# Squared norms of keys and queries: the factor goes into the square, and every square is made on ScalarE

## The chip, the cores and the metric

The kernel runs on one core of a Trainium2 chip. The metric is device time in microseconds (us). Three runs of the kernel before took 877.32, 878.21 and 878.77 us; their median, 878.21 us, is the time before. The profile comes from one more execution, which took 880.48 us.

## The reference

Three stages follow each other: attention with random features, and two feed-forward layers on its output.

```
scale = 1 / sqrt(sqrt(64))
q_s, k_s = q * scale, k * scale             # (4, 8, 576, 64)
def phi(x):                                 # omega: (128, 64)
    proj = einsum('bhsd,md->bhsm', x, omega)
    sq = sum(x * x, axis=-1) / 2
    h = proj - sq;  h = h - max(h)
    return exp(h) / sqrt(128)
kv, z = phi(k_s)^T v, sum_s phi(k_s)
x = (phi(q_s) kv) / (phi(q_s) . z + 1e-6)   # to (2304, 512)
h = x w1_in;  g = max(0.01 h, h);  x = g w1_out
h = x w2_in;  g = h * clip(h + 3, 0, 6) / 6;  out = g w2_out
```

What is changed here is `sq`: half of the squared norm of the scaled row, one number per token and head.

## The kernel before, in words

The 2304 tokens are cut into five groups of 512, 256, 512, 512 and 512. Three kinds of work share the engines. Attention comes in units: a key unit or a query unit of one head pair (or of several, for short pieces). The first feed-forward layer (moe1) runs group by group, while the attention of the next group is made beside it. The second layer (moe2) runs at the end; its weights are unpacked and converted earlier, beside the rest. A product of the feed-forward layers is three matmuls, L496, L497 and L498 (high times high, low times high, high times low), since each operand is kept as a high and a low part.

A unit of attention goes like this. DMAs bring the rows twice, transposed (`xT`) and by token (`xn`). TensorE makes the scores from `xT` (L739, L760). `squares` makes the squared norms from `xn`: a square in place (L674 on GpSimd or L675 on ScalarE), a sum over 64 columns on VectorE (L677), and a multiplication by half of scale squared, `halve` (L681, on VectorE or GpSimd). `features` takes the minimum of the scores on VectorE (L704), adds the norm on VectorE (L707), takes it away on VectorE or GpSimd (L710), and ScalarE makes the exponentials with the result as bias (L715). TensorE then makes keys times values (L786 in the first two batches) or transposes and multiplies with the result. The queries of the first group follow `Q_first`: transposes (L853), numerators (L862), a division on VectorE (L867 to L871), a transpose back (L880), and a split into high and low (L883 on ScalarE, L884 on VectorE), which gives the first operand `x` of moe1. Until those four `x` are there, moe1 can't begin. This first stretch, to about 47 us, is called the head below.

The weights come as 64-bit numbers and are turned into 32-bit ones by four steps (L519 or L521, L523, L526, L529), three of them on VectorE, and then split into high and low (L476 or L477, L480 or L481).

No order is written out by hand. `Graph.op` records each operation with a due time, its tiles, and one or more ways to do it: an engine, a cost in nanoseconds and the code. `Graph.run` then plans: at each step it takes the operation that can start first by its own clock of each engine (ties within 60 ns go to the earlier due time), picks for it the way that ends first, and emits it. The engines run what they are given in that order. The costs are those of `c_dve`, `c_act` and `c_pool`; `halve` stands in the table with 71 ns on VectorE and 200 ns on GpSimd. A way that is marked with `True`, or that runs on GpSimd, also holds the planner's clock `port`, one for both engines; `halve` on VectorE is not marked. Where the planner sees TensorE idle in the head for over 0.4 us, it fills half of the gap with matmuls on zeros (L1359, `keep_warm`).

Of the kernel before, what the change touches and what calls it, by code (L numbers as in the profile page):

```python
# [12 lines left out]
AF = mybir.ActivationFunctionType  # L13
ALU = mybir.AluOpType
# [311 lines left out]
def c_dve(n):  # L326
    return n / 0.96 + 69.0
# [6 lines left out]
def c_act(n, psum=False, ap=False):  # L334
    return n / 1.2 + (51.0 if psum else 93.0) + (93.0 if ap else 0.0)


def c_pool(n):
    return n * 2.1 + 147.0
# [11 lines left out]
def attn_moe_kernel(ctx: ExitStack, tc: tile.TileContext, qT, kT, qn, kn, v1, om2, w1i, w1o, w2i, w2o, out):  # L351
# [4 lines left out]
    nc = tc.nc  # L356
    scale = float(D) ** -0.25
    g = Graph()
# [141 lines left out]
    def dma(dst, src, nbytes):  # L500
        return [("sp", c_dma(nbytes), lambda: nc.sync.dma_start(dst(), src))]
# [166 lines left out]
    def squares(ncol, nsrc, due, nh=1):  # L668
        nat, sq = Buf("xn"), Buf("sq")
        N = lambda: nat.tiles[0][:, 0:ncol]  # L670
        to = (lambda: N().rearrange("p (h c) d -> p h c d", h=nh)) if nh > 1 else N
        g.op(dma(to, nsrc, 128 * ncol * 256), wr=[nat], due=due - O2)
        w = ncol * 64
        g.op([("pool", c_pool(w), lambda: nc.gpsimd.tensor_tensor(out=N(), in0=N(), in1=N(), op=ALU.mult)),  # L674
              ("act", c_act(w), lambda: nc.scalar.activation(N(), N(), AF.Square))], wr=[nat], due=due - 3e3)  # L675
        sqc = lambda: sq.tiles[0][:, 0:ncol]
        g.op([("dve", c_dve(w), lambda: nc.vector.tensor_reduce(out=sqc()[:, :, 0], in_=N(), axis=AX.X, op=ALU.add))],  # L677
             rd=[nat], wr=[sq], due=due - 2e3)

        def halve(eng):  # L680
            eng.tensor_scalar(out=sqc(), in0=sqc(), scalar1=0.5 * scale * scale, scalar2=None, op0=ALU.mult)  # L681

        g.op([("dve", 71, lambda: halve(nc.vector)), ("pool", 200, lambda: halve(nc.gpsimd))], wr=[sq], due=due - 2e3)
        return sq

    def exps(raw, h, nm, c, p, due):
# [61 lines left out]
    def K_tail(b, due):  # L748

        sq = squares(HP, kn[b, :, :, 8].rearrange("h p d -> p h d"), due)  # L750
        src, p, h = Buf("xT"), Ps(g.use), Buf("ht")
        last64[b] = h
        g.op(dma(lambda: src.tiles[0][:, 0:HP * 64].rearrange("p (h t) -> p h t", h=HP), kT[b, :, :, 512:576].rearrange(
            "h p t -> p h t"), 128 * HP * 256), wr=[src], due=due - O2)

        def mm():
            for hp in range(HP):
                for e in range(2):
                    r = slice(64 * e, 64 * e + 64)
                    nc.tensor.matmul(p.tiles[0][r, hp * 128:hp * 128 + 128], lhsT=src.tiles[0][r, hp * 64:hp * 64 + 64], rhs=wn[r],  # L760
                                     start=True, stop=True)

        g.op([("pe", HP * 224.0, mm)], rd=[src], wr=[p], also=[h], due=due, mode="S")
        features([p], [h], [HP], [0], sq, due)
# [669 lines left out]
```

## Time and profile before

| what | value |
|---|---|
| median of three runs | 878.21 us |
| the profiled execution | 880.48 us |
| its span, first to last instruction | 878.5 us |
| TensorE matmul busy | 858.8 us (98%) |
| VectorE busy | 688.0 us (78%) |
| ScalarE busy | 486.6 us (55%) |
| GpSimd busy | 195.7 us (22%) |
| mean granted TensorE clock | 0.998 |

The profiled execution took 2.0 us more than its span, which is what lies ahead of the first and behind the last instruction, and 2.27 us more than the median. A busy share says little here by itself: TensorE's matmuls overlap, so that a busy TensorE need not be at its full pace, and the other engines are far busier in the first 350 us, where all of attention lies, than behind it.

### The profile page before, as it was taken

The page shows a single profiled execution, that of the slowest core. Times are in us where ns is not written, and L with a number is a line of the kernel's source. Part 1 is how long each engine was busy: PE and PEld are TensorE (multiplying, and loading weights), DVE is VectorE, ACT ScalarE, POOL GpSimd, SP SyncE. Part 2 cuts the span into 40 slices and gives each one's busy share as a digit, 9 for nine tenths or more (in the row PEclk, how much of TensorE's full clock was granted, in tenths as well). Part 3 has the DMA queues.
Part 4 walks back from the last instruction along what each step waited for, and adds up shares of the span by engine and source line. Part 5 has one row for each costly group of instructions (what it writes and reads, how often), then busy time and mean ns, then how long its engine had stood idle before and what let it go on. Part 6 is the DMA issues. An engine that isn't in the chain of part 4 may idle for free.

```text
span 878.5 us, 17799 instructions
## 1 busy us (share of the span) xinstructions
PE 858.8 (98%) x6339; PEld 781.6 (89%) x6339; DVE 688.0 (78%) x1712; ACT 486.6 (55%) x1132; POOL 195.7 (22%) x334
## 2 busy tenths in 40 slices
PE   8999899999999999999999999999999999999998
PEld 8978787889878878888888888999999999999998
DVE  6999999898998877666688445788678779878865
ACT  7867566676767556554555345544453355445442
POOL 2322222535444412200100001121102303121200
PEclk9999999999999999999999999999999999999999
DMA  9556564668468564799898448884887675677352
GB/s 330 170 174 196 164 209 136 212 210 253 118 183 266 166 192 156 258 372 340 321 355 337 161 150 265 308 303 164 275 292 255 220 268 165 212 261 260 115 160 64
DMA packets 91496, 198.00 MB, mean 225 GB/s; under 512 B 14736, under 2 KB 40976, under 8 KB 91408
## 3 DMA queue, kind: packets, MB, share of 16 engines
q1 hardware_dynamic: 91408, 196.87, 66.6%
q8 instruction: 50, 0.82, 0.4%
q14 instruction: 38, 0.31, 0.1%
HBM read 150.18 MB, written 46.66 MB: 224 GB/s over the span
## 4 chain that ended last, share of the span: by engine, by line
PE 68%; DVE 16%; DMA 7%; ACT 4%; issue 3%; POOL 1%; SPq 1%; DVEq 0%; ACTq 0%; POOLq 0%
PE bank L1062 18%; PE bank L1162 16%; PE bank L496 9%; PE bank L497 9%; PE bank L498 9%; DVE wst L526 2%; DVE nm L704 2%; PE bank L739 2%; DVE junk L910 2%; ACT h L715 2%; DMA late_w<-in 1%; DVE g L1004 1%; DMA third_w<-in 1%; DMA out_raw<-wt 1%; DVE wst L523 1%
## 5 line engine op out<-in xcount | busy, mean ns | idle before, releaser
L1062 PE MATMUL bank<-w,g 128*128 128x256 f32 x720 | 95.9, 275 | 0.5 <-ACT bank L1195 0.3
L1062 PEld LDWEIGHTS bank<-w,g 128*128 128x128 f32 x720 | 87.9, 192 | 1.0 <-ACT bank L1195 0.4
L477 ACT COPY late_u<-bank 128x256 f32<-128x256 f32 (+1 forms) x103 | 39.7, 388 | 86.4 <-PE bank L1162 77.4
L1004 DVE TENSOR_TENSOR g<-bank,g 128x512 fp32r<-128x512 f32 (+1 forms) x80 | 50.9, 637 | 34.7 <-ACT g L477 34.2
L1002 ACT ACTIVATE bank<-bank 128x512 f32<-128x512 f32 (+1 forms) x80 | 44.2, 553 | 55.9 <-PE bank L498 55.8
L715 ACT ACTIVATE h<-bank,nm 128x128 f32<-128x128 f32 x228 | 63.7, 385 | 19.0 <-POOL nm L710 18.7
L496 PE MATMUL bank<-x,w 128*128 128x512 f32 (+1 forms) x180 | 67.0, 372 | 0.3 <-ACT h L715 0.3
L1162 PE MATMUL bank<-x,late_w 128*128 128x256 f32 x528 | 66.7, 275 | 0.0
L496 PE MATMUL bank<-g,w 128*128 128x512 f32 (+1 forms) x180 | 66.7, 371 | 0.0
L498 PE MATMUL bank<-g,w 128*128 128x512 f32 (+1 forms) x180 | 64.7, 359 | 2.0 <-DVE g L1004 1.9
L1162 PE MATMUL bank<-second_w,late_w 128*128 128x256 f32 x474 | 64.7, 275 | 0.9 <-ACT late_u L477 0.5
L497 PE MATMUL bank<-x,w 128*128 128x512 f32 (+1 forms) x180 | 64.5, 358 | 0.0
L498 PE MATMUL bank<-x,w 128*128 128x512 f32 (+1 forms) x180 | 64.5, 358 | 0.0
L497 PE MATMUL bank<-g,w 128*128 128x512 f32 (+1 forms) x180 | 64.5, 358 | 0.0
L1162 PEld LDWEIGHTS bank<-x,late_w 128*128 128x128 f32 x528 | 62.8, 192 | 0.2
L1162 PEld LDWEIGHTS bank<-second_w,late_w 128*128 128x128 f32 x474 | 58.9, 192 | 1.5 <-ACT late_u L477 0.7
L704 DVE TENSOR_REDUCE nm<-bank 128x4 f32<-128x512 f32 (+2 forms) x76 | 48.1, 660 | 3.9 <-PE bank L739 2.8
L710 POOL TENSOR_TENSOR nm<-nm,sq 128x4 f32<-128x4 f32 (+2 forms) x76 | 27.2, 368 | 100.1 <-DVE nm L707 98.2
L921 POOL TENSOR_TENSOR h<-h,den 128x512 f32<-128x512 f32 (+2 forms) x32 | 35.8, 1120 | 52.0 <-DVE den L916 29.7
L496 PE MATMUL bank<-x,second_w 128*128 128x512 f32 (+1 forms) x120 | 44.5, 371 | 1.4 <-ACT h L715 1.4
L480 DVE TENSOR_TENSOR g<-xr,g 128x384 fp32r<-128x384 f32 (+1 forms) x53 | 33.7, 636 | 14.3 <-ACT g L477 13.9
L910 DVE CUSTOM_DVE_ANT_0 junk<-h,zr 128x128 bf16<-128x128 f32 (+1 forms) x128 | 42.8, 374 | 1.0 <-ACT h L715 0.3
(373 smaller groups left out, 2393.6 us busy)
## 6 DMA issues: line engine op xcount, KB each, us to landing
late_w<-in SPq DMA_DIRECT2D x85, 512.0 KB, 4.5
in<-late_w SPq DMA_DIRECT2D x32, 512.0 KB, 4.2
late_w<-in SPq DMA_DIRECT2D x39, 256.0 KB, 5.0
third_w<-in SPq DMA_DIRECT2D x19, 512.0 KB, 4.6
wst<-w2i SPq DMA_DIRECT2D x16, 512.0 KB, 4.5
wst<-w2o SPq DMA_DIRECT2D x16, 512.0 KB, 4.2
x_t<-late_w SPq DMA_DIRECT2D x12, 512.0 KB, 5.3
wst<-w1i SPq DMA_DIRECT2D x10, 512.0 KB, 4.6
```

The lines of the kernel that those rows point to most:

```text
L477: return [("act", c_act(n, psum), lambda: nc.scalar.copy(dst(), src())), dve if psum else dve + (True,)]
L496: nc.tensor.matmul(o, lhsT=ah, rhs=bh, start=start, stop=False)
L497: nc.tensor.matmul(o, lhsT=al, rhs=bh, start=False, stop=False)
L498: nc.tensor.matmul(o, lhsT=ah, rhs=bl, start=False, stop=stop)
L704: g.op([("dve", c_dve(c * 128), lambda raw=raw, n_=n_: nc.vector.tensor_reduce(out=n_()[:, :, 0], in_=raw(), axis=AX.X, op=ALU.min))], rd= ...
L715: nc.scalar.activation(h.tiles[0][:, q * 128:q * 128 + 128], raw()[:, q], AF.Exp, bias=nm.tiles[0][:, q], scale=-1.0)
L910: nc.vector.tensor_tensor_reduce(out=jk.tiles[0][r, q % 2], in0=h.tiles[0][r, q * 128:q * 128 + 128], in1=zr[k].tiles[0][r, e], scale=1.0, ...
L921: eng.tensor_tensor(out=x, in0=x, in1=den.tiles[1][:, 0:c].to_broadcast([128, c, 128]), op=ALU.mult)
L1002: g.op([("act", c_act(n, True), lambda: nc.scalar.activation(P(), P(), AF.Prelu, alpha=0.01))], wr=[p], due=d)
L1004: g.op([("dve", c_dve(n), lambda: nc.vector.tensor_tensor(out=G1(), in0=P(), in1=G0().bitcast(F32), op=ALU.subtract))], rd=[p, (gg, 0)], w ...
L1062: nc.tensor.matmul(acc[bank].tiles[0][:, half * 256:half * 256 + 256], lhsT=src.tiles[x][:, q * 128:q * 128 + 128], rhs=woven(w[k].tiles[y ...
L1162: nc.tensor.matmul(R[r](), lhsT=w[x], rhs=m[y], start=start and k == n == 0, stop=k == 1 and n == 2, skip_group_check=True)
```

## The change

`halve` goes. Its factor, half of scale squared, is taken into the square: ScalarE's activation computes the square of its input times a scale, and the scale is now the root of that factor. The way on GpSimd goes too, since a plain product has no place for the factor, so that all squares are made on ScalarE.

```
-        g.op([("pool", c_pool(w), lambda: nc.gpsimd.tensor_tensor(out=N(), in0=N(), in1=N(), op=ALU.mult)),
-              ("act", c_act(w), lambda: nc.scalar.activation(N(), N(), AF.Square))], wr=[nat], due=due - 3e3)
+        g.op([("act", c_act(w), lambda: nc.scalar.activation(N(), N(), AF.Square, scale=scale * 0.5 ** 0.5))], wr=[nat], due=due - 3e3)
         sqc = lambda: sq.tiles[0][:, 0:ncol]
         g.op([("dve", c_dve(w), lambda: nc.vector.tensor_reduce(out=sqc()[:, :, 0], in_=N(), axis=AX.X, op=ALU.add))],
              rd=[nat], wr=[sq], due=due - 2e3)
-
-        def halve(eng):
-            eng.tensor_scalar(out=sqc(), in0=sqc(), scalar1=0.5 * scale * scale, scalar2=None, op0=ALU.mult)
-
-        g.op([("dve", 71, lambda: halve(nc.vector)), ("pool", 200, lambda: halve(nc.gpsimd))], wr=[sq], due=due - 2e3)
         return sq
```

There are 41 squares. Before, 35 were on ScalarE and 6 on GpSimd; of the 41 `halve`, 10 were on VectorE and 31 on GpSimd. Since the planner's clocks run differently without them, everything from the second pair of units on is planned anew: on TensorE the order is the old one for the first 28 rows of 3375, and again for the last 1701. In the changed kernel, lines from 678 on have numbers that are lower by six (L715 is L709, L862 is L856), and the square and the sum are L674 and L676.

The first place is ScalarE at about 16 us, behind the exponentials of the first query unit (`first_h_5`). `first_xn_0` and `first_xn_1` are the rows by token of the second key unit and of its query unit; `h_0_145` and `h_0_146` are the exponentials of that key unit. Before:

```order
L715 ACTIVATE first_h_5_0_163<-bank_182,nm_0_118 128x128 x4
L675 ACTIVATE first_xn_1_0_169<-first_xn_1_0_169 128x512
L477 COPY zr_0_134<-bank_181 128x256
L521 ACTIVATE first_wt_0_0_174<-first_wst_0_0_172 128x512
L715 ACTIVATE h_0_145<-bank_179,nm_0_119 128x128 x4
L715 ACTIVATE h_0_146<-bank_180,nm_0_120 128x128 x4
```

And now:

```order
L709 ACTIVATE first_h_5_0_163<-bank_182,nm_0_118 128x128 x4
L674 ACTIVATE first_xn_0_0_168<-first_xn_0_0_168 128x512
L477 COPY zr_0_134<-bank_181 128x256
L674 ACTIVATE first_xn_1_0_169<-first_xn_1_0_169 128x512
L521 ACTIVATE first_wt_0_0_174<-first_wst_0_0_172 128x512
L521 ACTIVATE first_wt_1_0_175<-first_wst_1_0_173 128x512
L709 ACTIVATE h_0_145<-bank_179,nm_0_119 128x128 x4
L784 COPY kvf_0_129<-bank_178 128x132
L709 ACTIVATE h_0_146<-bank_180,nm_0_120 128x128 x4
```

The square of `first_xn_0`, which GpSimd made before, now stands here, and a second weight conversion (L521) as well.

The second place is VectorE at the same time: the minima and norms of the two units, and the copies of the first unit's transposes (`first_tq`). Before:

```order
L707 TENSOR_TENSOR nm_0_118<-nm_0_118,sq_0_124 128x4
L677 TENSOR_REDUCE sq_0_125<-first_xn_0_0_168 128x8
L476 COPY first_tq_0_0_171<-bank_177 128x512
L476 COPY first_tq_0_0_171<-bank_178 128x512
L704 TENSOR_REDUCE nm_0_119<-bank_179 128x4
L704 TENSOR_REDUCE nm_0_120<-bank_180 128x4
L867 TENSOR_SCALAR den_0_188<-bank_176 128x4
L707 TENSOR_TENSOR nm_0_119<-nm_0_119,sq_0_125 128x4
```

And now:

```order
L701 TENSOR_TENSOR nm_0_118<-nm_0_118,sq_0_124 128x4
L476 COPY first_tq_0_0_171<-bank_177 128x512
L476 COPY first_tq_0_0_171<-bank_178 128x512
L698 TENSOR_REDUCE nm_0_119<-bank_179 128x4
L698 TENSOR_REDUCE nm_0_120<-bank_180 128x4
L861 TENSOR_SCALAR den_0_188<-bank_176 128x4
L676 TENSOR_REDUCE sq_0_125<-first_xn_0_0_168 128x8
L863 RECIPROCAL den_1_189<-den_0_188 128x4
L676 TENSOR_REDUCE sq_0_126<-first_xn_1_0_169 128x8
L865 TENSOR_TENSOR u_0_116<-bank_176,den_1_189 128x4x64
L861 TENSOR_SCALAR den_0_190<-bank_177 128x4
L701 TENSOR_TENSOR nm_0_119<-nm_0_119,sq_0_125 128x4
```

The sum over `first_xn_0` has moved from ahead of the two copies to behind the minima, and the sum over `first_xn_1` follows it ahead of the first addition to `nm_0_119`.

The third place is TensorE at the end of the head, up to the first matmul of moe1. `first_h_4` is the last exponential of the last query unit, `tq` its transposes, `u_0_117` its result. Before:

```order
L797 MATMUL bank_176<-ident,kvf_0_131 128x128 x2
L1359 MATMUL bank_183<-zero 128x384 x3
L853 MATMUL bank_182<-ident,first_h_4_0_162 128x128 x4
L862 MATMUL bank_177<-kvf_0_131,tq_0_154 128x66 x4
L862 MATMUL bank_180<-kvf_0_131,tq_0_154 128x66 x4
L1359 MATMUL bank_183<-zero 128x384 x8
L880 MATMUL bank_178<-ident,u_0_117 128x128 x4
L739 MATMUL bank_179<-wn,xT_0_140 64x128 x8
L496 MATMUL bank_176<-x_101,w_83 128x512
```

And now:

```order
L847 MATMUL bank_180<-ident,first_h_4_0_162 128x128 x4
L1353 MATMUL bank_183<-zero 128x384 x2
L856 MATMUL bank_177<-kvf_0_131,tq_0_154 128x66 x4
L874 MATMUL bank_178<-ident,u_0_116 128x128 x4
L856 MATMUL bank_176<-kvf_0_131,tq_0_154 128x66 x4
L1353 MATMUL bank_183<-zero 128x384 x9
L874 MATMUL bank_181<-ident,u_0_117 128x128 x4
L733 MATMUL bank_179<-wn,xT_0_140 64x128 x8
L496 MATMUL bank_180<-x_101,w_83 128x512
```

The result of the third query unit (`u_0_116`) is now transposed between the two numerator products of the fourth, and there are 40 matmuls on zeros in the head where there were 35.

## Rows read from the trace of the kernel before

**Rows 1.** Busy time by stretch: us, then each engine, granted clock, DMA, GB/s.
```profile
100.00:120.00 20.00, 17.49 (x104) 14.37 (x102) 19.84 (x50) 13.55 (x33) 7.35 (x9) 1.00 0.54 170
360.00:400.00 40.00, 40.00 (x187) 35.04 (x186) 25.38 (x56) 21.23 (x45) 3.71 (x5) 1.00 0.97 364
```
**Rows 2.** TensorE in order of time, end of the head: start, us, instruction, idle before.
```profile
40.51 2.11 PE L862 MATMUL bank<-kvf,tq 128*128 128x66 f32 x16 [0.42 <-ACT tq L477]
42.43 1.66 PE L1359 MATMUL bank<-zero 128*128 128x384 f32 x8
45.53 0.66 PE L880 MATMUL bank<-ident,u 128*128 128x128 f32 x4 [1.43 <-DVE u L871]
...
47.13 0.48 PE L496 MATMUL bank<-x,w 128*128 128x512 f32 x1
```
**Rows 3.** TensorE in order of time, where both kernels' orders meet again.
```profile
359.20 0.48 PE L496 MATMUL bank<-g,third_w 128*128 128x512 f32 x1
```
**Rows 4.** Squares on GpSimd and `halve`: count, duration ns min/median/max, first and last start.
```profile
L674 POOL TENSOR_TENSOR xn<-xn x5: 609/1036/1127, 26.5 to 265.0; 128x256 f32<-128x256 f32 x3, 128x512 f32<-128x512 f32 x2
...
L674 POOL TENSOR_TENSOR first_xn<-first_xn x1: 1040/1040/1040, 12.3 to 12.3; 128x512 f32<-128x512 f32 x1
...
L681 POOL TENSOR_SCALAR sq<-sq x31: 223/233/1212, 4.6 to 292.1; 128x8 f32<-128x8 f32 x20, 128x4 f32<-128x4 f32 x4, 128x7 f32<-128x7 f32 x4, 128x6 f32<-128x6 f32 x3
L681 DVE TENSOR_SCALAR sq<-sq x10: 158/719/999, 29.1 to 305.0; 128x8 f32<-128x8 f32 x5, 128x6 f32<-128x6 f32 x3, 128x4 f32<-128x4 f32 x2
```
**Rows 5.** ScalarE in order of time, in the head.
```profile
16.91 0.82 ACT L675 ACTIVATE first_xn<-first_xn 128x512 f32<-128x512 f32 x1
17.55 0.44 ACT L477 COPY zr<-bank 128x256 f32<-128x256 f32 x1
17.82 0.74 ACT L521 ACTIVATE first_wt<-first_wst 128x512 f32<-128x512 f32 x1
19.12 2.17 ACT L715 ACTIVATE h<-bank,nm 128x128 f32<-128x128 f32 x8 [0.55 <-POOL nm L710]
...
28.85 1.22 ACT L715 ACTIVATE h<-bank,nm 128x128 f32<-128x128 f32 x4
...
46.22 0.59 ACT L883 CAST x<-bank 128x512 fp32r<-128x512 f32 x1 [1.29 <-PE bank L880]
```
**Rows 6.** VectorE in order of time, in the head.
```profile
13.49 0.68 DVE L677 TENSOR_REDUCE sq<-first_xn 128x8 f32<-128x512 f32 x1
15.38 1.29 DVE L476 COPY first_tq<-bank 128x512 f32<-128x512 f32 x2 [1.22 <-PE bank L853]
```
**Rows 7.** ScalarE's groups from 10 to 47 us: count, busy us, mean ns, idle before.
```profile
L675 ACT ACTIVATE xn<-xn 128x512 f32<-128x512 f32 x4 | 2.7, 674 | 0.3 <-DMA xn<-kn 0.3
```
**Rows 8.** GpSimd and VectorE at one `halve`, in order of time.
```profile
104.56 1.14 POOL L921 TENSOR_TENSOR h<-h,den 128x512 f32<-128x512 f32 x1 [2.44 <-ACT xn L675]
...
104.73 1.00 DVE L681 TENSOR_SCALAR sq<-sq 128x6 f32<-128x6 f32 x1
```
**Rows 9.** VectorE's groups from 47 to 140 us.
```profile
L526 DVE SCALAR_TENSOR_TENSOR wst<-wst 128x512 uint32<-128x512 uint32 x14 | 11.7, 833 | 0.1
...
L529 DVE SCALAR_TENSOR_TENSOR wt<-wt,wst 128x512 uint32<-128x512 uint32 x9 | 6.8, 760 | 0.1
L523 DVE TENSOR_SCALAR wst<-wst 128x512 uint32<-128x512 uint32 x13 | 6.7, 512 | 0.2
...
L681 DVE TENSOR_SCALAR sq<-sq 128x6 f32<-128x6 f32 (+1 forms) x5 | 3.8, 762 | 0.1
```
**Rows 10.** What TensorE waited for, 47 to 359 us: us, times, longest.
```profile
PE bank L498 <- DVE g L1004: 1.9, 1, 1.9
PE bank L496 <- ACT h L715: 1.7, 2, 1.4
```
**Rows 11.** Busy time by stretch, where the granted clock (third number from the end) fell.
```profile
138.00:139.00 1.00, 1.00 (x4) 0.81 (x3) 1.00 (x2) 0.42 (x1) 0.00 (x0) 0.50 0.24 81
139.00:140.00 1.00, 1.00 (x3) 0.79 (x3) 1.00 (x3) 0.22 (x1) 0.00 (x0) 0.50 0.00 0
```

## The prediction

> **What bounds the kernel now.** I read the stretches first. From 360 to 400 us TensorE is busy for all of 40 us while VectorE is busy for 25; from 100 to 120 us VectorE is busy for 19.84 of 20 and TensorE for 17.49 [rows 1]. So there are two regimes: a late one in which only TensorE counts, and an early one, with attention beside the weight conversions, in which VectorE ends the waits. Then I asked where the change can act at all. The last square lies near 300 us, and TensorE's order is the old one again from the matmul that starts at 359.20 us [rows 3]. Behind it nothing is gained or lost by the change itself: the time moves by as much as the start of that matmul moves.
>
> Ahead of it I looked at two things in order of time. The head: TensorE works through it almost without a gap, and its end hangs on a chain of ScalarE and VectorE: the numerators wait 0.42 us for the copy of the transposes, the last transpose waits 1.43 us for VectorE's `u` in spite of eight matmuls on zeros, and moe1 starts at 47.13 us [rows 2]. From there to 359 us the waits of TensorE are few: the two largest families, for VectorE's eviction `g` and for ScalarE's exponentials, are 1.9 and 1.7 us [rows 10]. That is nearly all that a lighter VectorE or GpSimd could give back between 47 and 359 us.
>
> **The change part by part.** *The squares.* Six squares of about 1.04 us (512 columns) or 0.61 us (256) leave GpSimd [rows 4] and go to ScalarE, where 512 columns take 0.67 us on average in the head [rows 7]. GpSimd is far from a bound, so that its time is worth nothing by itself. In the head ScalarE is what they stand in line for. The factor costs nothing: an activation with a scale is already there in L521, 0.74 us against 0.82 us for a square without one in the same stretch [rows 5].
>
> *The head, step by step.* I walk the new order with the durations of before.
> (1) GpSimd made the second key unit's square at 12.3 us [rows 4], so that VectorE could sum it at 13.49, in front of a gap of 1.22 us in which it waits for TensorE [rows 6]. Now the square is ScalarE's first piece of work behind the exponentials, at 16.91, and the next one follows at about 17.8. Each takes 0.64 us to the next start and the copy between takes 0.27 [rows 5]; they end at 17.6 and 18.4. The gap is lost to VectorE, and both sums (0.6 us each) now stand behind the first denominator at 18.5 and ahead of the additions. These come at about 20.4, GpSimd's subtraction at 20.6, and the exponentials of the second key unit at 20.9 instead of 19.12 [rows 5]: 1.8 us late. TensorE doesn't feel it yet, since it has other work until 23.3.
> (2) The lateness stays on ScalarE and VectorE, with two more conversions and three more squares in their queues before the third key unit is done. The exponentials that started at 28.85 [rows 5] need additions that VectorE reaches at 30.1, and stand behind a copy that needs a product of TensorE of 30.4; they start at 30.6. Here TensorE begins to wait, and the planner has put 1 and 5 matmuls on zeros there.
> (3) From here each step is late by what ScalarE still has in front of it: the numerators of the last unit start at about 42.0 instead of 40.51, and `u` is ready at 47.1 to 47.6, so that the last transpose comes 1.6 to 2.1 us behind its 45.53 [rows 2]. What is queued behind it is all of moe1.
> I take +1.9 us. The lower end is the five added matmuls on zeros alone, at 0.2 us each by the eight that take 1.66 us: +1.0. The upper end is all that ScalarE gets in the head: five squares, three copies (the two for `first_tq` and one for `zr`) and one conversion, nine pieces, all priced as the 0.67 us square, 6.1 us, less the 1.29 us that it idles ahead of its last cast [rows 5]: +4.8. The walk, which is nearer to the lower end, decides.
>
> *VectorE from 47 to 140 us.* Five of the ten `halve` of VectorE lie here, 3.8 us of busy time, 762 ns each, for something that takes 158 ns when nothing is in its way [rows 4, 9]. The rest is waiting: the one at 104.73 lasts 1.00 us and ends as GpSimd's multiplication ends, at 105.70 [rows 8]. Does the waiting go with the instruction? Mostly the next one inherits it: what follows on VectorE is mostly a reciprocal or a conversion step, which work on the same memory.
> The Trainium skill (SBUF — State Buffer, "Who interferes with whom") says that VectorE's second port pair is GpSimd's only one, that it is held for a whole instruction, and that a plain reduction never needs it while a copy, a `tensor_scalar` or an operation with two inputs in SBUF can. The 1.00 us agrees with it. By that rule only a `halve` in front of a reduction or a PSUM read gives its wait back; counted so, five would give 0.8 us for sure and 3.8 at the most.
> The planner fills the place, too. Up to the eighth eviction of moe1 (the one TensorE waits 1.9 us for), VectorE's new list has two more of each of L526 and L529, three more of L523 and of L519, three casts and one subtraction fewer, and four `halve` fewer. With L519 and the casts priced as L523 (they cancel) and the subtraction as L529, that is 2 x 0.83 + 1 x 0.76 + 3 x 0.51 = +3.95 us against 4 x 0.76 = 3.05 [rows 9]. Net +0.9; neighbours on VectorE overlap by about 0.09 us each (a sum of 0.68 us holds the next one up by 0.6), and the list is two instructions longer, which leaves +0.7. Its ends are -3.05 (the list would have to be as short as the removed rows) and +3.95 (all waits inherited).
>
> *From 140 to 359 us.* The last four `halve` and two squares on GpSimd go. The conversions that were drawn forward are missing here, so that by the end VectorE's list is shorter by all its `halve`. But TensorE is at its own pace for most of this stretch, and no more can come back than the 1.7 us that it waits for exponentials, which VectorE's minima and additions feed [rows 10]. Between 0 and -1.7 I take the middle, -0.8. GpSimd's 31 `halve`, 0.23 us each when free [rows 4], stood beside VectorE's work; I count them in the same term, at nothing else.
>
> *Sum:* +1.9 +0.7 -0.8 = +1.8 us: 882.3 us on the profiled execution's 880.48, and 880.0 us on the median, which is 2.27 us lower.
>
> **The rivals.** *Paid back.* VectorE and GpSimd are freed in the stretch where they end the waits, and the head's loss returns. For it: 3.8 us on the busiest engine, waits at the very place, and a loss of clock: for all of 138 to 140 us the granted clock is 0.50, the lower level of 1.2 GHz, which costs 1.0 us in these two microseconds, behind a wait of TensorE [rows 11]. Against it: the planner has given the room to conversions. If both families of waits and that clock loss went, it is +1.9 - 3.6 - 1.0 = -2.7: 875.5 us, faster. It decides from a return of 3.7 us on.
> The Trainium skill (Perfetto Trace Analysis, "Optimizing Scalar/DVE Operations") advises handing VectorE's work to ScalarE where VectorE is saturated, and warns that GpSimd is no such help since the two share a port; by this rule the change is right in kind, and the result would be this rival's. The 19.84 of 20 us agree with its condition.
> *A new stall.* The plan is new up to 359 us: one more wait like the 1.9 us at the eighth eviction, with a further microsecond at the lower clock behind it, makes +1.8 +2.9: 882.9 us. For it: from 100 to 120 us VectorE has 0.16 us of slack in 20, and conversions now stand ahead of evictions that stood behind them. Against: only one wait of that length is among those of before, and behind 360 us VectorE has 15 us of slack in 40 [rows 1, 10].
> *Nothing is left.* The head's loss is covered by slack, or the walk is wrong by a unit's order: 878.2 us. For it: TensorE waited 1.43 us there before, too. That the change would not do what it says I give nothing: the squares were on ScalarE 35 times before.
>
> **How the numbers follow.** My forecast (the head's loss stays, +0.6 to +3.2 us) gets 0.50, paid back 0.22, a new stall 0.18, nothing left 0.10. About 0.2%, 1.76 us, is what a measurement of this kernel can tell from no change. The forecast lies astride that bound at 879.97: half of it counts as same, half as slower. Faster: 0.22, less 0.02 for a return that falls short: 0.20. Same: 0.25 + 0.10 + 0.02 = 0.37. Slower: 0.25 + 0.18 = 0.43. The range goes from 876.2, most of the paid-back case's way, to 883.0, the new stall and the head's upper end; the forecast's own is 878.8 to 881.4.
>
> **What would show it.** In the changed profile the exponentials of the second key unit start near 20.9 us and those of the third near 30.6; the first L496 starts near 49.0 instead of 47.13; the eighth eviction comes about 2 us later than before; and from the matmul at 359.20 on, every time is shifted by one and the same amount. A first L496 at or ahead of 47.5 would break the head's term. An early L496 and a shift of zero is the last rival; a late one and a shift below -1.8 is the first, and then I expect fewer VectorE instructions over 0.9 us between 47 and 140. A stretch at the lower clock other than the one near 138 us speaks for the new stall.

## The result, and the profile after

The changed kernel takes 884.85 us (median of four runs, 883.17 to 886.37), the kernel before 878.47 (four runs, 877.32 to 878.77): a ratio of 1.0063, interval 1.0044 to 1.0082. It is slower by 6.4 us, where 1.8 were forecast, and lies above the whole range. The profiled execution took 884.65 us, with a span of 882.6. Each kernel has one profiled execution, which can lie off its median: by 2.0 us here before, and by -3.9 (e10) to +2.7 us (e15) among the runs below. Busy time, after:

```profile
PE 860.6 (98%) x6344; PEld 782.3 (89%) x6344; DVE 683.2 (77%) x1696; ACT 490.1 (56%) x1142; POOL 177.1 (20%) x299
```

VectorE has 4.8 us less to do than before, GpSimd 18.6 less, ScalarE 3.5 more, and the time went up. So the loss isn't in the amount of work on these engines; it has to be read from when TensorE waits. The stretches of [rows 1], after:

```profile
360.00:400.00 40.00, 39.94 (x183) 33.70 (x183) 23.14 (x52) 18.41 (x39) 2.29 (x3) 1.00 0.88 327
100.00:120.00 20.00, 17.88 (x89) 14.03 (x88) 18.59 (x48) 11.76 (x31) 8.29 (x8) 0.91 0.51 168
```

The two regimes are the same: behind 360 us only TensorE counts. From 100 to 120 us VectorE is not so full as before (18.59 for 19.84 us).

*The head.* ScalarE in order of time, as in [rows 5]:

```profile
17.87 0.86 ACT L674 ACTIVATE first_xn<-first_xn 128x512 f32<-128x512 f32 x1
18.39 0.60 ACT L477 COPY zr<-bank 128x256 f32<-128x256 f32 x1
18.64 0.88 ACT L674 ACTIVATE first_xn<-first_xn 128x512 f32<-128x512 f32 x1
...
21.30 1.14 ACT L709 ACTIVATE h<-bank,nm 128x128 f32<-128x128 f32 x4 [0.67 <-POOL nm L704]
...
31.14 0.27 ACT L784 COPY kvf<-bank 128x132 f32<-128x132 f32 x1 [1.43 <-PE bank L780]
31.30 0.90 ACT L709 ACTIVATE h<-bank,nm 128x128 f32<-128x128 f32 x3
```

The two squares stand where the walk put them, the second key unit's exponentials start at 21.30 (forecast 20.9), the third's at 31.30 (30.6), behind the copy that the walk named. TensorE at the end of the head, as in [rows 2]:

```profile
42.54 1.11 PE L856 MATMUL bank<-kvf,tq 128*128 128x66 f32 x8 [1.20 <-ACT tq L477]
...
44.74 1.81 PE L1353 MATMUL bank<-zero 128*128 128x384 f32 x9
47.80 0.66 PE L874 MATMUL bank<-ident,u 128*128 128x128 f32 x4 [1.24 <-DVE u L865]
...
49.41 0.48 PE L496 MATMUL bank<-x,w 128*128 128x512 f32 x1
```

The numerators come at 42.54 (forecast 42.0), the last transpose at 47.80 (47.1 to 47.6), the first L496 at 49.41: 2.27 us later than before.

*To 140 us.* The eighth eviction starts at 106.45 us, 3.3 later than before. What TensorE waited for between the head and 140 us: before (47.1 to 139.6 us), 4.3 us in all,

```profile
PE bank L498 <- DVE g L1004: 1.9, 1, 1.9
PE bank L786 <- ACT h L715: 1.2, 1, 1.2
PE bank L739 <- DVE g L1004: 0.6, 1, 0.6
```

and after (49.4 to 142.4 us), 4.6:

```profile
PE bank L498 <- DVE g L998: 1.8, 2, 1.0
PE bank L733 <- DVE g L998: 1.2, 1, 1.2
PE bank L496 <- DVE g L998: 1.0, 1, 1.0
```

The waits for evictions rose from 2.5 to 4.0 us, in four places instead of two, and the 1.2 us for exponentials went. The stretch at the lower clock of [rows 11] has moved; it comes behind the wait of 1.2 us (at 112 us) and again holds two full microseconds at 0.50:

```profile
114.00:115.00 1.00, 1.00 (x4) 0.77 (x3) 1.00 (x2) 0.00 (x0) 0.97 (x1) 0.50 0.70 242
115.00:116.00 1.00, 1.00 (x4) 0.82 (x3) 1.00 (x5) 0.00 (x0) 0.90 (x2) 0.50 1.08 418
```

The 101st L496 starts at 142.49 us, before at 139.65: 2.84 us late.

*To the matmul of [rows 3].* It is the 381st L496 and starts 5.29 us late:

```profile
364.49 0.38 PE L496 MATMUL bank<-g,third_w 128*128 128x512 f32 x1
```

So between these two matmuls, the 101st L496 and this one, 2.45 us more are lost. What TensorE waited for there, us in all, times, longest; first before (139.6 to 359.2 us), with 3.5 us in all:

```profile
PE bank L496 <- ACT h L715: 1.7, 2, 1.4
PE bank L936 <- ACT ht L715: 0.5, 1, 0.5
PE bank L967 <- DVE g L1004: 0.4, 1, 0.4
...
```

and after (142.4 to 364.4 us), with 5.3:

```profile
PE bank L498 <- DVE g L998: 1.6, 2, 0.9
PE bank L498 <- DVE x L480: 1.4, 1, 1.4
PE bank L930 <- issue: 1.0, 1, 1.0
PE bank L828 <- issue: 0.8, 1, 0.8
PE bank L496 <- ACT u L477: 0.3, 1, 0.3
PE bank L930 <- ACT xr L477: 0.2, 1, 0.2
```

The waits that the forecast hoped to give back did go: what ScalarE ends fell from 2.8 to 0.5 us. Others took their place: what VectorE ends rose from 0.4 to 3.0, and waits for which the profile shows no cause (`issue`) from 0.3 to 1.8; what ended those stays open. All waits together rose by 1.8 of the 2.45 us. Yet VectorE does less in this stretch (third engine; before, then after):

```profile
139.60:359.20 219.60, 216.02 (x1603) 179.37 (x1602) 191.44 (x541) 142.90 (x388) 85.51 (x142) 1.00 0.62 191
```

```profile
142.40:364.40 222.00, 216.47 (x1604) 179.01 (x1603) 186.54 (x529) 145.38 (x393) 72.28 (x121) 1.00 0.62 188
```

It is idle for 35.5 us instead of 28.2. Where it idles shows in its groups of the same two stretches (busy us, mean ns, idle before); before:

```profile
L704 DVE TENSOR_REDUCE nm<-bank 128x4 f32<-128x512 f32 (+2 forms) x47 | 28.9, 644 | 2.4 <-PE bank L739 2.0 <-PE bank L760 0.3
...
L1004 DVE TENSOR_TENSOR g<-bank,g 128x512 fp32r<-128x512 f32 (+1 forms) x35 | 19.7, 567 | 10.6 <-ACT g L477 10.5
L523 DVE TENSOR_SCALAR wst<-wst 128x512 uint32<-128x512 uint32 x34 | 18.0, 528 | 5.5 <-ACT wt L521 5.2
```

and after:

```profile
L698 DVE TENSOR_REDUCE nm<-bank 128x4 f32<-128x512 f32 (+2 forms) x47 | 29.1, 644 | 9.5 <-PE bank L733 9.5
...
L998 DVE TENSOR_TENSOR g<-bank,g 128x512 fp32r<-128x512 f32 (+1 forms) x36 | 20.4, 568 | 4.2 <-ACT g L477 4.0
L523 DVE TENSOR_SCALAR wst<-wst 128x512 uint32<-128x512 uint32 x33 | 16.8, 509 | 9.2 <-ACT wt L521 8.9
```

Before, VectorE waited most in front of the evictions themselves, ready for them. Now it waits in front of minima (9.5 us, before 2.4) and conversions (9.2 us, before 5.5). That this idle time makes TensorE wait isn't shown: in the last microsecond ahead of each of the three waits for VectorE, it is at work. GpSimd, VectorE and TensorE at the longest, after, in order of time:

```profile
245.43 0.26 DVE L904 CUSTOM_DVE_ANT_0 junk<-h,zr 128x128 bf16<-128x128 f32 x1
...
245.61 0.29 DVE L904 CUSTOM_DVE_ANT_0 junk<-h,zr 128x128 bf16<-128x128 f32 x1
245.65 1.15 POOL L915 TENSOR_TENSOR h<-h,den 128x512 f32<-128x512 f32 x1 [0.41 <-DVE den L910]
...
245.84 1.11 DVE L904 CUSTOM_DVE_ANT_0 junk<-h,zr 128x128 bf16<-128x128 f32 x1
...
247.29 1.89 DVE L480 TENSOR_TENSOR x<-xr,x 128x512 fp32r<-128x512 f32 x2
...
248.00 0.48 PE L498 MATMUL bank<-x,w 128*128 128x512 f32 x1 [1.42 <-DVE x L480]
```

The two instructions of L904 just ahead take 0.26 and 0.29 us; this one takes 1.11 and ends 0.15 us behind GpSimd's product, which ends at 246.80, as at the `halve` of [rows 8]. The other two waits are of the same kind:

```profile
169.23 0.93 POOL L915 TENSOR_TENSOR h<-h,den 128x384 f32<-128x384 f32 x1 [1.81 <-DVE den L910]
169.41 0.89 DVE L904 CUSTOM_DVE_ANT_0 junk<-h,zr 128x128 bf16<-128x128 f32 x1
...
170.71 0.38 PE L498 MATMUL bank<-g,w 128*128 128x256 f32 x1 [0.76 <-DVE g L998]
...
339.25 1.15 POOL L915 TENSOR_TENSOR h<-h,den 128x512 f32<-128x512 f32 x1 [3.25 <-DVE den L910]
339.44 1.11 DVE L904 CUSTOM_DVE_ANT_0 junk<-h,zr 128x128 bf16<-128x128 f32 x1
...
341.43 0.48 PE L498 MATMUL bank<-g,second_w 128*128 128x512 f32 x1 [0.88 <-DVE g L998]
```

By their excess over 0.29 us, the three L904 account for some 2.2 of the 3.1 us (an estimate). They aren't more frequent than before: 13 of the 112 in this stretch take over 0.7 us, before 14. The new order puts three of them ahead of what TensorE needs next.

Behind the 400th L496 the lag is 5.5 us for 200 of them in a row. The execution of before then loses more to late transfers, 2.6 us behind 500 us:

```profile
PE bank L1162 <- DMA late_w<-in: 1.5, 3, 0.9
PE bank L1162 <- DMA third_w<-in: 1.1, 2, 0.6
```

where the changed one has only the first of the two families, also 1.5. That is 1.1 of the 1.4 us by which the lag falls to the end: its span is 4.1 us longer.

### The profile page after: what moved, and what is told of

The parts are those of the page before. It is cut to its first block, busy times and chain, and to the rows that moved or that the text cites. A ratio compares the mean times of both kernels' runs of the same rounds, so it can differ in the third digit from the quotient of the medians.

```text
span 882.6 us, 17764 instructions
## 1 busy us (share of the span) xinstructions
PE 860.6 (98%) x6344; PEld 782.3 (89%) x6344; DVE 683.2 (77%) x1696; ACT 490.1 (56%) x1142; POOL 177.1 (20%) x299
## 4 chain that ended last, share of the span: by engine, by line
PE 66%; DVE 15%; DMA 8%; ACT 5%; issue 3%; SPq 1%; POOL 0%; DVEq 0%; ACTq 0%; POOLq 0%
PE bank L1056 18%; PE bank L1156 16%; PE bank L496 9%; PE bank L498 9%; PE bank L497 9%; DMA in_raw<-wt 2%; DVE g L998 2%; PE bank L733 2%; DVE junk L904 2%; DVE wt L529 2%; DVE wst L526 2%; DMA late_w<-in 2%; DVE nm L698 1%; ACT h L709 1%; DMA out_raw<-wt 1%
## 5 line engine op out<-in xcount | busy, mean ns | idle before, releaser
L709 ACT ACTIVATE h<-bank,nm 128x128 f32<-128x128 f32 x228 | 64.7, 386 | 21.2 <-POOL nm L704 20.6
L498 PE MATMUL bank<-g,w 128*128 128x512 f32 (+1 forms) x180 | 65.0, 361 | 2.7 <-DVE g L998 2.6
L496 PE MATMUL bank<-x,w 128*128 128x512 f32 (+1 forms) x180 | 66.5, 369 | 1.0 <-DVE g L998 1.0
L496 PE MATMUL bank<-g,w 128*128 128x512 f32 (+1 forms) x180 | 66.8, 371 | 0.3 <-ACT u L477 0.3
L498 PE MATMUL bank<-x,w 128*128 128x512 f32 (+1 forms) x180 | 64.6, 359 | 1.4 <-DVE x L480 1.4
L521 ACT ACTIVATE wt<-wst 128x512 f32<-128x512 f32 x40 | 32.6, 821 | 26.5 <-DMA out_raw<-wt 12.2
L496 PE MATMUL bank<-x,second_w 128*128 128x512 f32 (+1 forms) x120 | 44.9, 374 | 0.0
L904 DVE CUSTOM_DVE_ANT_0 junk<-h,zr 128x128 bf16<-128x128 f32 (+1 forms) x128 | 43.8, 380 | 0.9 <-ACT h L709 0.2
```

The lines of the kernel that those rows point to most:

```text
L496: nc.tensor.matmul(o, lhsT=ah, rhs=bh, start=start, stop=False)
L498: nc.tensor.matmul(o, lhsT=ah, rhs=bl, start=False, stop=stop)
L709: nc.scalar.activation(h.tiles[0][:, q * 128:q * 128 + 128], raw()[:, q], AF.Exp, bias=nm.tiles[0][:, q], scale=-1.0)
L904: nc.vector.tensor_tensor_reduce(out=jk.tiles[0][r, q % 2], in0=h.tiles[0][r, q * 128:q * 128 + 128], in1=zr[k].tiles[0][r, e], scale=1.0, ...
```

## Experiments

The theories, with the words that the expectations use. *Work*: something that the change issues (five or six squares more on ScalarE in the way, no `halve`) costs the time. *Order* or *chance*: the work is worth next to nothing; the planner's new order has other waits, and another order would have others again. *Rules*: orders that the planner makes without `halve` are slow as a class. *Head* or *early*: the late first L496 decides, or the order up to 165 us.

All timed runs stand in one table: is `halve` in the plan (also an empty one, which issues nothing), the time over that of the kernel before with its interval, and, from one profiled execution, the start of the first L496, the lag of the 401st L496 against the profile of before, and what TensorE waited for from 47 to 366 us (the sum of the rows of that view; where the head ends later than 47 us, its last wait is in it). Numbers are those of the labels.

| kernel | planned `halve` | ratio | first L496 | lag, 401st | waits |
|---|---|---|---|---|---|
| before | yes | 1 | 47.13 | 0 | 7.8 |
| after | no | 1.0063 (1.0044 to 1.0082) | 49.41 | +5.5 | 11.2 |
| e1 | empty | 0.9996 (0.9986 to 1.0007) | 47.81 | -1.7 | 5.9 |
| e2 | yes, most empty | 0.9992 (0.9981 to 1.0003) | 46.94 | -1.4 | 6.8 |
| e3 | no | 1.0088 (1.0071 to 1.0105) | 48.91 | +6.8 | 10.5 |
| e4 | yes | 1.0002 (0.9989 to 1.0015) | 47.20 | +1.3 | 7.7 |
| e5 | empty, to 165 us | 1.0012 (1.0001 to 1.0023) | 47.99 | +1.0 | 7.5 |
| e6 | empty, from 165 us | 1.0040 (1.0020 to 1.0059) | 48.75 | +5.1 | 10.5 |
| e7 | no | 1.0079 (1.0059 to 1.0099) | 48.73 | +6.6 | 11.1 |
| e8 | yes | 0.9982 (0.9969 to 0.9994) | 47.75 | -1.7 | 7.3 |
| e9 | no | 1.0114 (1.0087 to 1.0141) | 46.61 | +12.4 | 14.9 |
| e10 | no | 1.0064 (1.0039 to 1.0088) | 46.79 | +2.0 | 9.7 |
| e11 | yes | 1.0019 (1.0008 to 1.0029) | 47.41 | +2.2 | 9.7 |
| e12 | no | 1.0056 (1.0041 to 1.0071) | 46.03 | +5.2 | 11.8 |
| e13 | empty | 1.0014 (0.9996 to 1.0033) | 47.06 | -2.0 | 6.0 |
| e14 | empty | 0.9983 (0.9970 to 0.9995) | 46.95 | -1.4 | 7.4 |
| e15 | empty | 1.0058 (1.0035 to 1.0081) | 47.02 | +7.7 | 13.8 |
| e16 | yes, most empty | 0.9968 (0.9956 to 0.9981) | 48.19 | -2.1 | 7.0 |
| e17 | no | 1.0031 (1.0020 to 1.0043) | 46.76 | +3.1 | 9.4 |
| e18 | no | 1.0023 (1.0013 to 1.0034) | 47.24 | +0.1 | 7.4 |

**Order or work: e1 to e4.** e1, the order of before with the work of after:

```
-        g.op([("pool", c_pool(w), <square on GpSimd>), ("act", c_act(w), <square>)], ...)
+        on_act = lambda: nc.scalar.activation(N(), N(), AF.Square, scale=scale * 0.5 ** 0.5)
+        g.op([("pool", c_pool(w), on_act), ("act", c_act(w), on_act)], ...)
-        g.op([("dve", 71, <halve>), ("pool", 200, <halve>)], ...)
+        g.op([("dve", 71, lambda: None), ("pool", 200, lambda: None)], ...)
```

> The planner sees what it saw before the change (two ways for the square, and a multiplication by the factor), so that every engine keeps the order of before; but what is emitted is the change's work: all 41 squares on ScalarE with the factor, each at the place of its old square, and nothing for the multiplications. Order theory (the loss is in the new order of instructions): TensorE's start of moe1 stays within 1 us of 47.1, and the time is 876 to 879 us. Work theory (ScalarE has no room for six more squares): the start of moe1 moves to about 49 us as in the changed kernel, and the time is 880 to 885.

It took 879.25 us, as long as the kernel before (879.7 beside it). The head is 0.67 us late instead of 2.27. That these 0.67 us are work (the moved squares) isn't shown: e8 below, with the order and the work of before up to there, is 0.62 us late as well. The rest is order.

e2, the order of before; `halve` isn't issued where ScalarE makes the square (35 of 41), the six squares stay on GpSimd and keep theirs:

```
+        ... AF.Square, scale=scale * 0.5 ** 0.5)   # on ScalarE; on GpSimd as before
+        ("dve", 71, lambda: plain and halve(nc.vector))   # plain: made on GpSimd
```

> The order of before, word for word; the six squares stay on GpSimd and keep their multiplication by the factor, the other 35 multiplications are gone, their factor in ScalarE's square. Work is only taken away, 9 instructions on VectorE and 26 on GpSimd. Order theory: 0 to 3 us faster than before, 875.5 to 878.5, since part of the waits that VectorE ends between 47 and 359 us goes. If the removed instructions pass on all their waits, it is within 1 us of before. Slower than before by over 1 us would speak against both.

878.45 us. The removal alone is worth 0 to 0.2%, and by the interval it may be nothing. e3, the order of after, and 41 `halve` back on VectorE, behind the sum, with no factor in the square:

```
+        nc.vector.tensor_scalar(out=sqc(), in0=sqc(), scalar1=0.5 * scale * scale, scalar2=None, op0=ALU.mult)
```

> The changed kernel's order, word for word, with 41 multiplications by the factor put back on VectorE, each right behind its sum, and no factor in the square. Order theory: as slow as the changed kernel or slower, 884 to 889 us (41 x 0.09 us at least, up to 0.66 each where GpSimd holds it up). If the changed kernel's loss had to do with the missing multiplications rather than with the order, it would come back towards 879.

886.88 us, with the loss of the changed kernel and some 2 us on top, perhaps for the 41 instructions (the two intervals overlap). The loss stays with the order whether the work is there or not. e4, only the squares are moved, `halve` kept:

```
-        g.op([("pool", ...), ("act", c_act(w), <square>)], ...)
+        g.op([("act", c_act(w), lambda: nc.scalar.activation(N(), N(), AF.Square))], ...)
```

> One part of the change alone: the squares may only go to ScalarE, the multiplication by the factor stays, and the planner plans anew. If this part is what costs the head (ScalarE gets four more squares there, TensorE waits at its end), moe1 starts at 48.5 to 50 us and the time is 880 to 886. If the loss comes from the plan's re-draw between 140 and 359 us, the start of moe1 says nothing on the time, which may be anything from 877 to 886.

880.13 us: a third order, and no loss. The work theory falls with e1 and e3.

**Which part of the order: e5 to e8.** e5 gives the planner the old ways (empty) for the attention of the first two groups only, e6 for the later groups only; both issue the work of after:

```
+        old = Buf.GRP <= 1                     # e6: Buf.GRP > 1
+        g.op([("pool", c_pool(w), on_act)] * old + [("act", c_act(w), on_act)], ...)
+        if old: g.op([("dve", 71, lambda: None), ("pool", 200, lambda: None)], ...)
```

> The work of the changed kernel throughout (all squares on ScalarE with the factor, no halve). Only what the planner is told differs: for the first two groups' attention it still believes in a way on GpSimd and in a halve that issues nothing, so that the order is that of the kernel before up to about 165 us (the 132nd L496); for the later groups it is told the truth. Theory 'chance' (a new order carries new stalls, one order as well as another, whatever the rules): up to the 132nd L496 as the run with the old order and the new work, about +0.4 us on before; behind that anything from -2 to +5. Rival 'rules' (the planner without halve and without the way on GpSimd packs VectorE so tightly that its orders are worse as a class): the +5 that the changed kernel gains between the 140th and the 400th L496 comes here too, so that from the 400th on the lag is +3 to +5, total 881.5 to 883.5. Rival 'head' (the late start of moe1 is what costs, and the rest follows from it): the first L496 near 47.8, lag from the 400th on between -1.7 and +0.5, total 878 to 879.5.

> The reverse of the last: the work of the changed kernel; the planner is told the truth for the first two groups' attention, so that the order is that of the changed kernel up to about 165 us (the 133rd L496), and has the false way and the empty halve for the later groups. First L496 near 49.4 and a lag of about +0.6 to +1 at the 130th L496 in every theory. 'Chance': behind that anything from -2 to +5. 'Rules': nothing more is lost, the lag from the 400th L496 on is 0 to +1.5, total 878 to 880.5. 'Head': the whole +4 to +5.5 shows again, total 882.5 to 885.

e5 is within 0.2% of before, and the new rules behind 165 us cost little there: at the 132nd L496, where its order leaves that of before, it is 0.4 us late, at the 401st 1.0. In e6 the 132nd is 2.1 us late and the 401st 5.1: it lost 3 us under the old rules, by these two waits among others:

```profile
200.02 0.33 PE L817 MATMUL bank<-ident,kvf 128*128 128x128 f32 x1 [1.19 <-ACT h L717]
201.09 0.67 PE L836 MATMUL bank<-zr,ones 128*128 128x256 f32 x2 [0.75 <-POOL zr L825]
```

In time it lies between the ranges of the rules and of the head theory. That speaks against the rules as such, and for the early order or chance. e7 and e8 leave the kernels after and before alone and turn one neutral number of the planner:

```
-    LAT = 165.0        # e7, on the kernel after
+    LAT = 170.0
-    NEAR = 60.0        # e8, on the kernel before
+    NEAR = 70.0
```

> The changed kernel, with one of the planner's own numbers moved: it takes 170 ns instead of 165 for the way of a result to another engine. The work is the same to the instruction, the rules are the same, the order is another from the 174th row of TensorE on. 'Chance': a time that is off the changed kernel's 884.85 by more than 1.8 us, to either side, most likely lower (878 to 883), since the changed kernel's order is then an unlucky one. 'Rules': 883 to 887. 'Head': the head's order stays nearly the same, first L496 at 48.5 to 49.5, total 883 to 886.

> The kernel before, with halve and the squares on GpSimd as they were, and one of the planner's own numbers moved: ties are those within 70 ns instead of 60. The order is the old one through the head and up to the 1386th row of TensorE, another one behind it. 'Chance': it can lose 1 to 5 us without any change of the work, and will more likely be slower than faster, 878 to 883. 'Rules' and 'head': within 1 us of the kernel before, 877.5 to 879.5.

e7 stays slow (885.8 us), e8, whose order is another only from about 250 us on, is 0.18% faster than before: against chance, which had e7 lower and e8 slower.

**Is it the head: e9 to e12.** e9 is the other half of the change: `halve` gone, squares still allowed on GpSimd. The six that GpSimd makes lack the factor, so this kernel leaves out a part of the work:

```
-        g.op([("dve", 71, <halve>), ("pool", 200, <halve>)], ...)
```

> One half of the change alone: halve is gone from the planner too, squares on ScalarE carry the factor, and squares may still go to GpSimd (those lack the factor, so what is left out here is the factor in a few of the squares). The counterpart, all squares on ScalarE with halve kept, has been run: 1.0002 of the kernel before, first L496 at 47.20. 'Rules': an order made without halve is worse, so this one shows most of the changed kernel's loss, first L496 at 48.5 or later, 881 to 885. 'Chance': the time says nothing of the half that is done, anything from 877 to 884. 'Head' (the second key unit's square behind ScalarE's exponentials is what makes the head late): GpSimd can make that square again, so the first L496 comes at 47.0 to 47.8.

> The changed kernel with ties within 70 ns instead of 60: the same work, the new rules, another order from TensorE's 60th row on. The kernel before with the same 70 took 0.9982 of its time with 60. 'Rules': 882.5 to 887, and 5 us or more behind the kernel before with 70. 'Chance': anything from 877 to 886; with three orders under the new rules all slow so far, I lean to slow. 'Early' (what costs is the order that the new rules give up to 165 us, its late first L496 above all): the time goes with the first L496: at 47.5 or sooner 877 to 880, at 48.5 or later 882 to 886.

> The kernel before with ties within 50 ns: the old rules and work, another order from TensorE's 90th row on, so in the head as well. 'Rules': within 2 us of the kernel before, 877 to 880.5, and at least 3 us ahead of the changed kernel with the same 50. 'Chance': anything from 877 to 886. 'Early': by the first L496 as above.

> The changed kernel with ties within 50 ns: the new rules, another order from TensorE's 100th row on. 'Rules': 882.5 to 887. 'Chance': anything from 877 to 886. 'Early': by the first L496, at 47.5 or sooner 877 to 880, at 48.5 or later 882 to 886.

e10 is after with `NEAR = 70.0`, e11 before with 50.0, e12 after with 50.0. The head theory falls: e12 has the earliest moe1 of all, and is slow. Its TensorE at the end of the head, and at its longest wait:

```profile
46.03 0.48 PE L496 MATMUL bank<-x,w 128*128 128x512 f32 x1
...
174.31 0.58 PE L496 MATMUL bank<-g,w 128*128 128x256 f32 x1 [2.35 <-ACT g L477]
```

1.1 us ahead in the head, and 2.35 gone in one wait. e9 has nearly the same wait, and the latest end of all, 890.54 us, beyond every range that it was given:

```profile
177.86 0.58 PE L496 MATMUL bank<-g,w 128*128 128x256 f32 x1 [2.21 <-ACT g L477]
```

By then all five orders planned throughout without `halve` (those of after and e3 are one) were slow, and all planned with it within 0.2%.

**Rules or chance: e13 to e18.** e13 to e15 are the changed kernel with an empty `halve` in the plan, e14 on GpSimd only, e15 with `NEAR = 70.0` beside:

```
+        g.op([("dve", 71, lambda: None), ("pool", 200, lambda: None)], wr=[sq], due=due - 2e3)
```

> All of the change's work, but the planner still plans a halve, which issues nothing. The order is row for row that of the run with all squares on ScalarE and halve kept (1.0002 of the kernel before). 'Rules' (an order planned without halve's claim on GpSimd and VectorE is the slow one): 878.5 to 881, with the first L496 at 46.8 to 47.8 and a lag of 0 to +1.5 from the 400th L496 on. 'Work' (something that the change issues costs time in itself): as the changed kernel, 883 to 886. 'Chance' says the same as 'rules' here, since the order is a known one.

> As the last, but the empty halve is planned on GpSimd only: another order, from TensorE's 28th row on against the changed kernel and from the 581st against the last run. 'Rules': within 0.3% of the kernel before, 877.5 to 882. 'Chance' (the five orders without halve were slow by luck): anything from 877 to 888.

> All of the change's work, an empty halve in the plan, and ties within 70 ns instead of 60: another order from TensorE's 60th row on. The changed kernel with 70 and without the empty halve took 1.0064 of the time of the kernel before. 'Rules': 877.5 to 882, at least 3 us less than that one. 'Chance': anything from 877 to 888.

e13 and e14 have all of the change and none of its loss; e14, 876.95 us, just under both ranges given for it, is faster than the kernel before by an interval that excludes 1. This is the plainest proof that the work of the change isn't what costs. e15 falls out: `halve` in the plan, and 0.58% slower, with an early head. So the empty `halve` is no cure.

What did the planner lose with `halve`? The order tells without a run: an empty one that only delays the norm, on no engine's clock, gives the order of after row for row; an empty one that delays nothing and only claims GpSimd's or VectorE's clock gives that of e13. It is the claim on the clocks, not the longer chain.

e16 is e8 with the edit of e2. e17 and e18 are after with `LAT = 160.0` and with `NEAR = 80.0`:

> The fastest order so far (the kernel before with ties within 70 ns, 0.9982), row for row, with the factor taken into the square wherever ScalarE makes it, so that 34 of the 41 halve or so are not issued. 'Work costs little': the step's own worth is that of the same edit in the order of the kernel before (0.9992 of it), so 0.997 to 0.9985, 876.5 to 878.5. Any theory in which the removal frees VectorE where TensorE waits for it: below 0.996.

> The changed kernel, planned with 160 ns for the way of a result to another engine instead of 165: the same work, no halve in the plan, another order from TensorE's 60th row on. 'Rules' in its weaker form (orders without halve are mostly slow): 882.5 to 890 for this and the next. 'Chance': one of the two at 881 or below. In either case the time goes with TensorE's waits between 47 and 366 us: up to 8 us of them, 881 or less; 10 us and more, 882 or more.

> The changed kernel, planned with ties within 80 ns: the same work, no halve in the plan, another order from TensorE's 60th row on. Expected as for the run with 160 ns: 'rules' 882.5 to 890, 'chance' one of the two at 881 or below, and the time by TensorE's waits between 47 and 366 us.

e16 is the fastest of all, 875.79 us, 0.7 under its range. Against e8, whose order it has, that is 0.14%, within the noise of the two. Seven `halve` are left in it of 41:

```profile
L687 POOL TENSOR_SCALAR sq<-sq x5: 223/243/615, 15.0 to 279.7; 128x4 f32<-128x4 f32 x3, 128x8 f32<-128x8 f32 x2
L687 DVE TENSOR_SCALAR sq<-sq x2: 172/611/1050, 30.1 to 257.3; 128x8 f32<-128x8 f32 x2
```

e17 (881.78 us) and e18 (880.38) are slower than before by 0.31 and 0.23%: between the two theories. e17 missed the 882.5 of the rules as well as the 881 of chance by under a microsecond; e18 came out as chance had it, by its waits too.

What holds over all rows of the table is the last column: over the twenty profiled executions the waits and the execution's own time go together with a correlation of 0.95, 1.6 us of time for each us of wait by the fitted line. With the medians of the kernels it is 0.85. The granted clock has a share in the 1.6: from 30 to 400 us TensorE spends 6.8 to 10.2 us at 0.50 in e3, e6, e7, e9 and e12, all slow, 3.4 in the kernels before and after, and none in e5, e8, e10, e11, e16 and e18. The slow orders don't share one wait: in e15 the largest family is for ScalarE's exponentials (4.4 us), in the changed kernel for VectorE's evictions. Of seven distinct orders without a planned `halve` all are slower than before by over 0.2% (0.23 to 1.14); of six with it (before with e1 and e2, e4 with e13, e8 with e16, e11, e14, e15) one is, e15. So the rules lean to slow orders: of the 42 pairs of an order without and one with, the one without is slower in 39 (the other three are e15 against e12, e17 and e18). Why, stays open: the work done by VectorE and ScalarE up to 165 us differs by no constant sign between the two kinds.

## Why the prediction was wrong

*The head: right.* Each station of the walk came within 0.7 us, +2.27 against +1.9. It had the order right and could, since the order was known. By the other executions part of the +2.27 is chance: moe1 begins at 46.94 to 48.19 us in the six with the head's order of before (before, e1, e2, e5, e8, e16) and at 48.73 to 49.41 in the four with the new one (after, e3, e6, e7), 1.3 us later on average. A share of the moved squares isn't clear of this spread.

*47 to 140 us: right in size, in part by luck.* +0.6 us measured, +0.7 forecast. The waiting of `halve` didn't go with it: VectorE has 19 instructions over 0.9 us in that stretch instead of 13. VectorE's part came out larger (1.5 us more of waits for evictions), and a wait of 1.2 us for exponentials, on which the step said nothing, went.

*140 to 359 us: the step that failed.* It was forecast at -0.8, "between 0 and -1.7", and measured +2.45 (one execution each). The step read what waits of before could go (1.7 us for exponentials, and they went) and never asked which new ones the new order brings; a bound of 0 above was an assumption. The reason given, that TensorE is at its own pace there and VectorE's list is shorter, was true of the work and beside the point: VectorE had 4.9 us less to do there and 7.3 us more idle time. As far as the rows show, what counts is which instruction stands ahead of the one that TensorE needs: the three drawn-out L904 alone are some 2.2 us by the estimate above. No run moves these three by themselves, and the 1.5 us more of `issue` waits have no known cause. By the work alone the term would have been about the forecast's range: in the old order the 101st L496 of e2 is 0.87 us early and the 381st 1.35, of e1 +0.42 and -1.70, which makes -0.5 and -2.1. These are single executions, and neither kernel's median is clear of the one before.

*From the profile to the median: the other half of the miss.* The forecast took off 2.27 us, which the profiled execution of before lay above its median. That of the changed kernel lay 0.2 below its own. The difference between the profiles is 4.2 us, 2.4 more than forecast; between the medians it is 6.4. A part of the 2.27 can be named: late transfers cost 2.6 us in the profile of before, 1.5 in that of after, and 1.0 and 1.2 in e1 and e2, which have the order of before. What they cost differs from one execution to the next, and should have come off the profile of before ahead of the sum.

*The rivals.* "A new stall" was the right one in kind, at 0.18: with 1.42 us its longest wait is shorter than the one it was priced by, there are several, and the profile of after shows no second stretch at the lower clock ahead of 880 us. Its price of 2.9 us stood for a single place in a plan that is new for some 1650 rows of TensorE. "Paid back" was wrong. Of the two families that it named, the one for ScalarE's exponentials went, but the one for VectorE's evictions ahead of L498 grew from 1.9 us in one place to 3.5 in four. The Trainium skill's advice on a saturated VectorE (Perfetto Trace Analysis, "Optimizing Scalar/DVE Operations") fits the sign of what the work is worth in an unchanged order, 0 to 0.2% by e1, e2 and e16 (against e8), none of the three clear of zero; the time followed the order.

## What to carry to other kernels

Where a planner sets the order, a small edit changes two things: the work, which can be priced from rows, and the draw of a new order, which can't. Here the work moves the time by -0.2 to 0% and the draw by -0.2 to +1.1%, so give the draw a spread of its own on both sides (it need not be even: orders without `halve` in the plan were all on the slow side), and judge the edit in the old order (leave an empty operation in the plan) before judging it in a new one. And take what only one execution shows, such as late transfers, off the profile before a difference is carried over to the medians.

## What the runs showed that was not expected

An engine can have less work, more idle time and still be waited for more: VectorE's idle time from 140 to 359 us rose from 28.2 to 35.5 us while the waits for it rose from 0.4 to 3.0. The idle time by itself isn't the reason: from 47 to 366 us VectorE is idle for 40.0 us in the changed kernel and for 40.2 in e13, which has about half of the waits (6.0 us for 11.2). And neutral numbers of the planner (a latency of 160 to 170 ns, a tie of 50 to 80 ns) move the changed kernel by 0.6%, from 1.0023 (e18) to 1.0079 (e7), with the same operations planned each time.
